# A fused attention and two feed-forward networks: sixteen weight loads issued ahead of the second block's q and k, with weight conversion and attention of block 0 placed anew

## The chip, the core and the metric

The kernel runs on one core of a Trainium2 chip. A core has five engines that run their own instruction streams and wait for each other through semaphores: TensorE (PE in the rows, its weight loads PEld), VectorE (DVE), ScalarE (ACT), GpSimd (POOL) and SyncE (SP), which here issues every DMA. The metric is the device time of one execution in microseconds (us), less is better.

## The reference

Attention over chunks of 64 tokens, a gated network and a second network:

```python
scores = scale * np.matmul(q_c, k_c.transpose(0, 1, 2, 4, 3))      # per chunk of 64, 8 heads
attn = np.exp(scores - np.max(scores, axis=-1, keepdims=True))
attn = attn / (np.sum(attn, axis=-1, keepdims=True) + 1e-09)
x = np.matmul(attn, v_c)                          # reordered to (4608 tokens, 512)
xn = x / np.sqrt(np.mean(x * x, axis=-1, keepdims=True) + 1e-06) * rms_g
g = xn @ w_gate                                   # 512 -> 1536
y = (g / (1.0 + np.exp(-g)) * (xn @ w_val)) @ w_out
h = y @ w_in                                      # 512 -> 2048
out = (h * np.clip(h + 3.0, 0.0, 6.0) / 6.0) @ w_out2
```

## The kernel before

**Blocks and steps.** The 4608 tokens are worked in nine blocks of 512. All nine go through the first network, then all nine through the second. In the first network a block has twelve steps f (0 to 11), one for each 128 columns of the hidden layer, and a step has three thirds, counted by hk from 0 to 35: the gate product (twelve matmuls of 128x512 into bank GB), the val product (twelve, into bank VB), and the down product of the step before (twelve, into four banks). Gate and val each hold one bank, so the gate product of a step can only start when VectorE has read the one before (L689), and a val product when VectorE has read the val before (L694). L580 on ScalarE and L581 on GpSimd split the product of the two into a high and a low part, which the down product of the next step reads.

**Weights.** The weights arrive as 64-bit floats. The matmuls run on a rounded 32-bit format (fp32r), three of them for one exact product: high weight by high input, low weight by high input, high weight by low input. So each weight is first made a 32-bit float by operations on its two words and then split into a high and a low part. The weights of the first network come in 36 pieces of 512 KB, in the order gate 0, val 0, out 0, gate 1 and so on: piece i belongs to step i // 3. A piece passes through five stages: a DMA into a raw tile (L131), `mag` on ScalarE (L138, the magnitude of the high word), `bits` on VectorE (L145, L147, L149, L153, the 32-bit float), `hi` on ScalarE (L160, the high part) and `lo` on GpSimd (L168, the rest). `Prep.step(2)` advances four pairs of pieces by one stage each; `Prep.fill` loads more pieces while the pool `wp` of 36 slots has room. Raw tiles, finished weights and the attention tiles of block 0 share that pool, so a load can wait for an earlier user of its slot.

**Start.** Attention of block 0 (four `Att` objects) and the first fourteen pieces are written out by hand in `START`; sixteen pieces are loaded there. After that, attention for block b + 1 is done inside block b of the first network by two `Pair` objects of 256 tokens each. Pair 2 and Pair 3 belong to block 1, Pair 4 is the first of block 2. `att_hook(b, hk)` places the steps of a pair: `turn` (two transposes of q and k on VectorE, L405 and L406; right after it the q and k of the next pair are loaded with 32 or 64 small DMAs, L391), `scores` (L418), `top`, `less` and `expo`, `total` and `share`, `trans_p` and `out_p`, `values` (L478) and `squares` (L501), then the load of the next v (L401). After two pairs `rms(b + 1)` normalizes the block's input: a matmul, a square root on ScalarE (L517), a reciprocal (L518) and four products (L521) on VectorE. `x_split` then splits the input into XH (L531, ScalarE) and XL (L533, VectorE and GpSimd), which the first gate product of the next block reads.

**What sets the order.** `manual_schedule` keeps the order in which the code is written: each engine takes its instructions in that order, and one that waits holds up all that stand behind it on its engine. SP's DMAs stand in one queue in that order too; besides, each of them waits on the semaphore of the eighth DMA before it, which that DMA sets when it has landed. `prep_hook(b, hk)` places the conversion of the remaining pieces: in block 0 the table `HKA` says in which thirds a step is made. The hooks stand behind each third's product: in third hk, first the matmuls and the VectorE product, then `att_hook`, then `prep_hook`.

Of the kernel before, what the change touches and what calls it, by code (L numbers as in the profile page):

```python
# [36 lines left out]
    square3 mean2 spread1 norm1 spread0 root2 squares3 mean3 wl2 inv2 root3 wh3 hi1 spread2 norm0 inv3 wm5  # L37
    norm2 hi2 lo1 spread3 hi0 lo2 norm3 hi3 lo3 wh4 wm6 lo0 wl3 wb5 wb6 wh5 wl4
""".split()
HKA = [2, 0, 0, 0, 2, 2, 0, 2, 0, 0, 2, 0, 2, 0, 2, 0, 0, 2, 2, 2, 0, 0, 2, 2, 2, 2, 2, 2, 0, 0, 2, 0, 0, 2, 0, 2]  # L40
HKB = [2, 2, 2, 2, 2, 2, 0, 2, 0, 2, 2, 0, 2, 0, 2, 0, 0, 2, 2, 2, 0, 2, 0, 2, 0, 0, 2, 2, 0, 2, 2, 2, 0, 0, 0, 0]


# [1 line left out]
def fused_kernel(  # L45
# [466 lines left out]
    def rms(blk):  # L512

        ps = PS[:, ATT, :]
        nc.tensor.matmul(ps, ones, sqs.pop(blk), start=True, stop=True)
        rt = at_p.tile([128, N], F32, tag="kT", name="rt")
        nc.scalar.activation(rt, ps, AF.Sqrt, scale=1.0 / DM, bias=eps)  # L517
        nc.vector.reciprocal(rt, rt)  # L518
        x = xf[blk]
        for c in range(KD):  # L520
            nc.vector.scalar_tensor_tensor(  # L521
                out=x[:, c, :], in0=x[:, c, :], scalar=g_sb[:, c:c + 1], in1=rt, op0=ALU.mult, op1=ALU.mult
            )
# [5 lines left out]
    def x_split(x):  # L529
        for c in range(KD):  # L530
            nc.scalar.copy(XH[:, c, :], x[:, c, :])  # L531
            e = nc.vector if c % 2 == 0 else nc.gpsimd
            e.tensor_tensor(XL[:, c, :], x[:, c, :], XH[:, c, :].bitcast(F32), op=ALU.subtract)  # L533


    def mm_up(bank, w, xs):
        ps = PS[:, bank, :]
        n = 3 * KD
        i = 0
        for wi, xi in ((0, 0), (1, 0), (0, 1)):  # L540
            for c in range(KD):
                nc.tensor.matmul(  # L542
                    ps, w[:, wi, c * 128:(c + 1) * 128], xs[c][xi], start=(i == 0), stop=(i == n - 1)
                )
                i += 1

    def mm_down_a(w, a, first, last):
        for m in range(KD):
            ps = PS[:, YB + m, :]
            wm = [w[:, z, m * 128:(m + 1) * 128] for z in range(2)]  # L550
            nc.tensor.matmul(ps, wm[0], a[0], start=first, stop=False)  # L551
            nc.tensor.matmul(ps, wm[1], a[0], start=False, stop=False)  # L552
        for m in range(KD):
            nc.tensor.matmul(PS[:, YB + m, :], w[:, 0, m * 128:(m + 1) * 128], a[1], start=False, stop=last)  # L554
# [22 lines left out]
    def split_act(t):  # L577
        hi = ah_p.tile([128, N], F32R, tag="ah", name="ah")
        lo = al_p.tile([128, N], F32R, tag="al", name="al")
        nc.scalar.copy(hi, t)  # L580
        nc.gpsimd.tensor_tensor(lo, t, hi.bitcast(F32), op=ALU.subtract)  # L581
        return hi, lo

    def y_store(b):
        for m in range(0, KD, 2):
            t = st_p.tile([128, 2, N], F32, tag="st", name="yst")
            nc.scalar.copy(t[:, 0, :], PS[:, YB + m, :])
            nc.vector.tensor_copy(t[:, 1, :], PS[:, YB + m + 1, :])
            nc.sync.dma_start(out=yd[b][:, m:m + 2, :], in_=t)
# [13 lines left out]
    def load_x2(b):  # L603
        xf[b] = xf_p.tile([128, KD, N], F32, tag="xf", name="xf")
        nc.sync.dma_start(out=xf[b], in_=yd[b])
# [7 lines left out]
    with tc.manual_schedule():  # L613
        a_pieces = [(kd, f) for f in range(FA) for kd in ("gate", "val", "out")]
        b_pieces = [(kd, f) for f in range(FB) for kd in ("in2", "out2")]

        prep_a, prep_b = Prep(a_pieces), Prep(b_pieces)


        first = [Att(i) for i in range(NTL)]  # L620
        for op in LOADS:
            if op[0] == "w":
                prep_a.load()
            elif op[0] == "q":
                first[int(op[1])].load_qk()
            else:
                first[int(op[1])].load_v()
        for op in START:
            if op[0] == "w":
                prep_a.token(op)  # L630
            else:
                first[int(op[-1])].run(op[:-1])
        sqs.pop(0)
        xf.pop(0)

        nxt = Pair(N // TP)
        nxt.load_qk()
        nxt.load_v()
        state = {"att": nxt}

        def att_hook(b, hk):

            if b + 1 >= NB:
                return
            f, o = divmod(hk, 3)
            t, g = divmod(f, 5)
            a = state["att"]
            if t == N // TP:
                if hk == 3 * f + 1 and g == 0:
                    rms(b + 1)  # L650
                return
            if (g, o) == (0, 1):
                a.run("turn")
                if a.i + 1 < NPR:
                    state["nxt"] = Pair(a.i + 1)
                    state["nxt"].load_qk()
            elif (g, o) == (1, 0):
                a.run("scores")
            elif (g, o) == (1, 1):
                a.run("top", "less", "expo")  # L660
            elif (g, o) == (2, 1):
                a.run("total", "share")
            elif (g, o) == (3, 1):
                a.run("trans_p", "out_p")
            elif (g, o) == (4, 1):
                a.run("values", "out_x", "square", "squares")
                if "nxt" in state:
                    state["att"] = state.pop("nxt")
                    state["att"].load_v()

        def prep_hook(b, hk):
            if b == 0 and not prep_a.done() and HKA[hk]:
                prep_a.step(HKA[hk])
                prep_a.fill(36)
            if b == NB - 1:
                if HKB[hk]:
                    prep_b.step(HKB[hk])
                prep_b.fill(hk)

        for b in range(NB):  # L680
            prev = None
            hk = 0
            if b == NB - 1:
                load_x2(0)
            for f in range(FA):
                mm_up(GB, W["gate", f], xs)
                s = sg_p.tile([128, N], F32, tag="sg", name="sg")
                nc.scalar.activation(s, PS[:, GB, :], AF.Sigmoid)  # L688
                nc.vector.tensor_tensor(s, s, PS[:, GB, :], op=ALU.mult)  # L689
                att_hook(b, hk)  # L690
                prep_hook(b, hk)
                hk += 1
                mm_up(VB, W["val", f], xs)
                nc.vector.tensor_tensor(s, s, PS[:, VB, :], op=ALU.mult)  # L694
                a = split_act(s)
                att_hook(b, hk)
                prep_hook(b, hk)
                hk += 1
                if prev is not None:
                    mm_down_a(W["out", f - 1], prev, f == 1, False)  # L700
                att_hook(b, hk)
                prep_hook(b, hk)
                hk += 1
                prev = a
            if b + 1 < NB:
                x_split(xf.pop(b + 1))
            else:
                x_split(xf.pop(0))
            mm_down_a(W["out", FA - 1], prev, False, True)
            y_store(b)  # L710

        for b in range(NB):
            prev = None
            if b + 1 < NB:
                load_x2(b + 1)
            for f in range(FB):
                bank = GB + f % 2
                if b == 0:
                    prep_b.fill(36)
                    prep_b.step(2)  # L720
                mm_up(bank, W["in2", f], xs)
                s = sg_p.tile([128, N], F32, tag="sg", name="sg")
                nc.scalar.activation(s, PS[:, bank, :], AF.Relu, bias=three)  # L723
                nc.vector.scalar_tensor_tensor(  # L724
                    out=s, in0=s, scalar=6.0, in1=PS[:, bank, :], op0=ALU.min, op1=ALU.mult
                )
                a = split_act(s)
                if prev is not None:
                    mm_down_b(W["out2", f - 1], prev, f == 1, False)
                prev = a  # L730
            if b + 1 < NB:
                x_split(xf.pop(b + 1))
            mm_down_b(W["out2", FB - 1], prev, False, True, b == NB - 1)
            o_store(b)
# [29 lines left out]
```

## Time and profile before

| | us |
|---|---|
| median of 3 runs (1868.18 to 1870.50) | 1869.09 |
| the profiled execution | 1870.38 |
| its span in the trace | 1868.6 |
| TensorE busy in the span | 1782.3 (95%) |
| VectorE, ScalarE, GpSimd busy | 727.0, 601.1, 542.4 |

The profiled execution is 1.3 us over the median, and 1.8 us of it lie outside the span of the trace. TensorE is busy nearly throughout; the slices of the page show its busy share under 90% only in the first five of forty (234 us) and in a short place near the middle where the second network's weights are converted. Block 0 of the first network lies in slices 1 to 4.

### The profile page before, as it was taken

What the parts mean: (1) busy time and instruction counts of PE and PEld (TensorE: products, weight loads), DVE (VectorE), ACT (ScalarE), POOL (GpSimd) and SP (SyncE); (2) the same over time, 40 slices, a digit from 0 to 9 for tenths busy, and PEclk for the clock granted to TensorE, in tenths of its full rate; (3) what the DMA queues carried; (4) which work ended last, traced back from release to release, by engine and by line L of the source; (5) the groups of instructions that cost most, each with busy time, mean ns of one, the idle gap of its engine ahead of it and who ended that gap; (6) DMA issues with size and microseconds to landing.
All of it is one profiled execution on the core that took longest, in us unless ns stands there. A gap on an engine that the chain in (4) does not pass through costs nothing.

```text
span 1868.6 us, 24155 instructions
## 1 busy us (share of the span) xinstructions
PE 1782.3 (95%) x9856; PEld 1457.4 (78%) x9856; DVE 727.0 (39%) x930; ACT 601.1 (32%) x899; POOL 542.4 (29%) x395
## 2 busy tenths in 40 slices
PE   5678999999999999999999889999999999999999
PEld 4556788888888888888887678888888888888887
DVE  7787534344353534335359951121212121212121
ACT  5344423233232323233234432222323232322222
POOL 3534322112121212112125652222223232323222
PEclk8789999999999999999999999999999999999999
DMA  9362211212212121212034410110101010101000
GB/s 249 78 170 70 49 31 44 41 28 49 40 40 45 39 44 26 51 36 46 12 102 153 142 55 1 46 36 10 46 0 46 1 46 1 45 1 46 0 23 23
DMA packets 225199, 93.88 MB, mean 50 GB/s; under 512 B 192960, under 2 KB 213440, under 8 KB 223936
## 3 DMA queue, kind: packets, MB, share of 16 engines
q1 hardware_dynamic: 225088, 92.34, 18.8%
q8 instruction: 77, 1.26, 0.3%
q14 instruction: 34, 0.28, 0.1%
HBM read 73.40 MB, written 18.87 MB: 49 GB/s over the span
## 4 chain that ended last, share of the span: by engine, by line
PE 82%; DVE 6%; SPq 3%; issue 3%; POOL 2%; DMA 2%; ACT 1%; DVEq 0%; POOLq 0%; ACTq 0%
PE PS L542 45%; PE PS L563 7%; PE PS L559 7%; PE PS L560 7%; PE PS L551 4%; PE PS L552 4%; PE PS L554 4%; SPq L391 2%; POOL w L168 2%; DVE wtmp L149 1%; DVE wraw L153 1%; PE PS L418 1%; DMA wraw<-in_moe_w_gate_dram 1%; PE PS L478 1%; DVE wtmp L145 1%
## 5 line engine op out<-in xcount | busy, mean ns | idle before, releaser
L542 PE MATMUL PS<-XH,w 128*128 128x512 f32 x2880 | 729.6, 396 | 41.8 <-DVE sg L689 29.4
L581 POOL TENSOR_TENSOR al<-sg,ah 128x512 fp32r<-128x512 f32 x252 | 334.0, 1325 | 1279.9 <-ACT ah L580 1279.9
L542 PEld LDWEIGHTS PS<-XH,w 128*128 128x128 f32 x2880 | 547.5, 191 | 163.9 <-DVE sg L689 33.7
L542 PE MATMUL PS<-XL,w 128*128 128x512 f32 x1440 | 389.0, 392 | 0.0
L724 DVE SCALAR_TENSOR_TENSOR sg<-sg,PS 128x512 f32<-128x512 f32 x144 | 99.2, 689 | 623.5 <-ACT sg L723 623.5
L542 PEld LDWEIGHTS PS<-XL,w 128*128 128x128 f32 x1440 | 273.8, 190 | 57.7
L580 ACT CAST ah<-sg 128x512 fp32r<-128x512 f32 x252 | 156.3, 620 | 429.6 <-DVE sg L694 313.9
L723 ACT ACTIVATE sg<-PS,three 128x512 f32<-128x512 f32 x144 | 99.1, 688 | 445.8 <-PE PS L542 431.5
L559 PE MATMUL PS<-w,ah 128*128 128x512 f32 x576 | 224.5, 390 | 2.8 <-ACT ah L580 2.8
L560 PE MATMUL PS<-w,ah 128*128 128x512 f32 x576 | 224.1, 389 | 0.0
L689 DVE TENSOR_TENSOR sg<-sg,PS 128x512 f32<-128x512 f32 x108 | 74.0, 685 | 274.7 <-ACT sg L688 274.6
L551 PE MATMUL PS<-ah,w 128*128 128x512 f32 x432 | 175.8, 407 | 0.2 <-ACT ah L580 0.2
L552 PE MATMUL PS<-ah,w 128*128 128x512 f32 x432 | 168.5, 390 | 0.0
L563 PE MATMUL PS<-w,al 128*128 128x512 f32 x576 | 154.9, 390 | 2.1 <-POOL al L581 2.1
L688 ACT ACTIVATE sg<-PS 128x512 f32<-128x512 f32 x108 | 64.4, 596 | 246.1 <-PE PS L542 229.5
L559 PEld LDWEIGHTS PS<-w,ah 128*128 128x128 f32 x576 | 108.1, 188 | 26.4 <-ACT ah L580 4.0
L563 PEld LDWEIGHTS PS<-w,al 128*128 128x128 f32 x576 | 108.2, 188 | 25.2 <-POOL al L581 2.9
L560 PEld LDWEIGHTS PS<-w,ah 128*128 128x128 f32 x576 | 108.2, 188 | 22.4
L694 DVE TENSOR_TENSOR sg<-sg,PS 128x512 f32<-128x512 f32 x108 | 74.2, 687 | 120.5 <-PE PS L542 117.1
L554 PE MATMUL PS<-al,w 128*128 128x512 f32 x432 | 115.8, 390 | 0.1
L168 POOL TENSOR_TENSOR w<-wraw,w 128x512 fp32r<-128x512 f32 x68 | 102.0, 1525 | 17.9 <-ACT w L160 17.9
L551 PEld LDWEIGHTS PS<-ah,w 128*128 128x128 f32 x432 | 81.1, 188 | 21.4 <-ACT ah L580 2.8
(85 smaller groups left out, 1229.0 us busy)
## 6 DMA issues: line engine op xcount, KB each, us to landing
wraw<-in_moe_w_out_dram SPq DMA_DIRECT2D x28, 512.0 KB, 5.2
yd<-yst SPq DMA_DIRECT2D x18, 512.0 KB, 3.4
xf<-yd SPq DMA_DIRECT2D x9, 1024.0 KB, 6.5
wraw<-in_moe_w_in_dram SPq DMA_DIRECT2D x16, 512.0 KB, 3.9
out_dram<-ost SPq DMA_DIRECT2D x16, 512.0 KB, 3.2
wraw<-in_moe_w_gate_dram SPq DMA_DIRECT2D x12, 512.0 KB, 6.5
wraw<-in_moe_w_val_dram SPq DMA_DIRECT2D x12, 512.0 KB, 7.4
v<-in_v_dram SPq DMA_DIRECT2D x96, 64.0 KB, 2.6
```

The lines of the kernel that those rows point to most:

```text
L168: nc.gpsimd.tensor_tensor(w[:, 1, :], self.raw.pop(i)[:, :, 0].bitcast(F32), w[:, 0, :].bitcast(F32), op=ALU.subtract)
L542: nc.tensor.matmul(ps, w[:, wi, c * 128:(c + 1) * 128], xs[c][xi], start=(i == 0), stop=(i == n - 1))
L551: nc.tensor.matmul(ps, wm[0], a[0], start=first, stop=False)
L552: nc.tensor.matmul(ps, wm[1], a[0], start=False, stop=False)
L554: nc.tensor.matmul(PS[:, YB + m, :], w[:, 0, m * 128:(m + 1) * 128], a[1], start=False, stop=last)
L559: nc.tensor.matmul(PS[:, YB + m, :], am, w[:, 0, :], start=first, stop=False)
L560: nc.tensor.matmul(PS[:, YB + m, :], am, w[:, 1, :], start=False, stop=False)
L563: nc.tensor.matmul(PS[:, YB + m, :], a[1][:, m * 128:(m + 1) * 128], w[:, 0, :], start=False, stop=last)
L580: nc.scalar.copy(hi, t)
L581: nc.gpsimd.tensor_tensor(lo, t, hi.bitcast(F32), op=ALU.subtract)
L723: nc.scalar.activation(s, PS[:, bank, :], AF.Relu, bias=three)
L724: nc.vector.scalar_tensor_tensor(out=s, in0=s, scalar=6.0, in1=PS[:, bank, :], op0=ALU.min, op1=ALU.mult)
```

## The change

Three edits, all in block 0 of the first network:

- All weight pieces that fit are loaded at once behind `START` (`fill(36, 36)`), before the q and k of Pair 2; the v of Pair 2 is loaded in third 0.
- `HKA` makes a conversion step in every second third (hk 0, 2, 4, ...), and `fill` is tried in every third.
- Attention of block 0 stands one step (three thirds) later: the first `turn` in third 4 and no longer in third 1, `rms` in third 34 and no longer in 31. The other blocks keep their places.

```diff
-HKA = [2, 0, 0, 0, 2, 2, 0, 2, 0, 0, 2, 0, 2, 0, 2, 0, 0, 2, 2, 2, 0, 0, 2, 2, 2, 2, 2, 2, 0, 0, 2, 0, 0, 2, 0, 2]
+HKA = [0 if hk % 2 else 2 for hk in range(36)]
...
+        prep_a.fill(36, 36)
         nxt = Pair(N // TP)
         nxt.load_qk()
-        nxt.load_v()
         state = {"att": nxt}
...
             f, o = divmod(hk, 3)
+            a = state["att"]
+            if b == 0:
+                if hk == 0:
+                    a.load_v()
+                    return
+                f -= 1
             t, g = divmod(f, 5)
-            a = state["att"]
+            if t < 0:
+                return
             if t == N // TP:
-                if hk == 3 * f + 1 and g == 0:
+                if o == 1 and g == 0:
                     rms(b + 1)
                 return
...
-            if b == 0 and not prep_a.done() and HKA[hk]:
-                prep_a.step(HKA[hk])
+            if b == 0 and not prep_a.done():
+                if HKA[hk]:
+                    prep_a.step(HKA[hk])
                 prep_a.fill(36)
```

Line numbers in the changed code from `att_hook` on are 8 higher (L689 becomes L697, L694 becomes L702).

SP's queue behind the last load of `START`, one piece of the difference (- before, + after); `wraw` are weight pieces, q, k and v those of the pairs:

```order
-L391 DMA q<-in_q_dram 32x2x32 x16
-L391 DMA q<-in_q_dram 32x6x32 x16
-L391 DMA k<-in_k_dram 32x2x32 x16
-L391 DMA k<-in_k_dram 32x6x32 x16
-L401 DMA v<-in_v_dram 64x64 x8
-L401 DMA v<-in_v_dram 64x3x64 x8
 L131 DMA wraw<-in_moe_w_val_dram 128x4x256
```

```order
+L131 DMA wraw<-in_moe_w_out_dram 128x1024
+L131 DMA wraw<-in_moe_w_gate_dram 128x4x256
+L131 DMA wraw<-in_moe_w_val_dram 128x4x256
+L391 DMA q<-in_q_dram 32x2x32 x16
+L391 DMA q<-in_q_dram 32x6x32 x16
+L391 DMA k<-in_k_dram 32x2x32 x16
+L391 DMA k<-in_k_dram 32x6x32 x16
```

The 64 DMAs for q and k of Pair 2 stood in front of the next weight piece; now sixteen pieces stand in front of them (the last three are shown).

VectorE in the first two steps of block 0, before:

```order
L689 TENSOR_TENSOR sg<-sg,PS 128x512
L694 TENSOR_TENSOR sg<-sg,PS 128x512
L405 STREAM_TRANSPOSE qT<-q 128x1024
L406 STREAM_TRANSPOSE kT<-k 128x1024
L689 TENSOR_TENSOR sg<-sg,PS 128x512
L694 TENSOR_TENSOR sg<-sg,PS 128x512
```

and after, the same place:

```order
L697 TENSOR_TENSOR sg<-sg,PS 128x512
L702 TENSOR_TENSOR sg<-sg,PS 128x512
L145 TENSOR_SCALAR wtmp<-wtmp 128x512 x2
L147 TENSOR_SCALAR wtmp<-wtmp 128x512 x2
L149 SCALAR_TENSOR_TENSOR wtmp<-wraw,wtmp 128x512 x2
L153 SCALAR_TENSOR_TENSOR wraw<-wraw,wtmp 128x512 x2
L697 TENSOR_TENSOR sg<-sg,PS 128x512
L702 TENSOR_TENSOR sg<-sg,PS 128x512
L405 STREAM_TRANSPOSE qT<-q 128x1024
L406 STREAM_TRANSPOSE kT<-k 128x1024
```

The transposes moved behind the products of step 1, and a pair of pieces is converted in front of them. From these transposes to those of Pair 3 VectorE has the same ten products L689 and L694 before and after, and six conversions of a pair before, eight after.

## Rows read from the trace of the kernel before

**Rows 1.** Busy time by stretch: stretch, length, busy us of each engine (instructions), PEclk, DMA, GB/s.
```profile
60.00:212.00 152.00, 117.50 (x694) 91.85 (x693) 113.29 (x149) 62.48 (x93) 64.05 (x44) 0.90 0.37 98
212.00:318.40 106.40, 106.06 (x707) 86.80 (x706) 44.84 (x52) 33.71 (x46) 22.62 (x17) 1.00 0.20 40
```
**Rows 2.** Waits in 60 to 212 us: who waited for whom, us in total, times, longest.
```profile
PE PS L542 <- DVE sg L689: 27.2, 7, 6.7
```
**Rows 3.** SP in order of time: start us, us until the last issue, issues.
```profile
40.55 19.58 SPq L391 DMA_DIRECT2D q<-in_q_dram  x32
60.17 15.50 SPq L391 DMA_DIRECT2D k<-in_k_dram  x32
...
141.96 16.28 SPq L391 DMA_DIRECT2D q<-in_q_dram  x32
158.34 15.08 SPq L391 DMA_DIRECT2D k<-in_k_dram  x32
173.60 0.35 SPq L131 DMA_DIRECT2D wraw<-in_moe_w_out_dram  x1
```
**Rows 4.** Chain of work that ended last, in order of time: start us, us, what.
```profile
40.14 7.13 DMA wraw<-in_moe_w_gate_dram
...
75.23 1.94 DMA k<-in_k_dram
77.19 1.26 DVE kT L406
78.49 1.99 PE PS L418 x64
...
117.46 10.15 DMA wraw<-in_moe_w_gate_dram
...
212.35 2.72 PE PS L542 x12
```
**Rows 5.** GpSimd in order of time, end of the start stretch: start us, us, what.
```profile
57.41 6.33 POOL L168 TENSOR_TENSOR w<-wraw,w 128x512 fp32r<-128x512 f32 x4
```
**Rows 6.** VectorE in order of time, block 0: start us, us, what [idle before <- releaser].
```profile
85.00 0.69 DVE L694 TENSOR_TENSOR sg<-sg,PS 128x512 f32<-128x512 f32 x1 [5.99 <-PE PS L542]
...
88.06 2.66 DVE L145 TENSOR_SCALAR wtmp<-wtmp 128x512 f32<-128x512 f32 x2
...
95.96 0.75 DVE L145 TENSOR_SCALAR wtmp<-wtmp 128x512 f32<-128x512 f32 x2
...
99.82 0.69 DVE L689 TENSOR_TENSOR sg<-sg,PS 128x512 f32<-128x512 f32 x1
...
115.30 0.69 DVE L689 TENSOR_TENSOR sg<-sg,PS 128x512 f32<-128x512 f32 x1 [3.62 <-ACT sg L688]
...
140.69 1.24 DVE L405 STREAM_TRANSPOSE qT<-q 128x1024 f32<-128x1024 f32 x1
...
189.40 0.67 DVE L689 TENSOR_TENSOR sg<-sg,PS 128x512 f32<-128x512 f32 x1
...
201.10 3.35 DVE L518 RECIPROCAL rt<-rt 128x512 f32<-128x512 f32 x1 [2.69 <-ACT rt L517]
204.49 2.74 DVE L521 SCALAR_TENSOR_TENSOR xf<-xf,g_sb,rt 128x512 f32<-128x512 f32 x4
...
209.83 3.14 DVE L533 TENSOR_TENSOR XL<-xf,XH 128x512 fp32r<-128x512 f32 x2 [1.21 <-ACT XH L531]
```
**Rows 7.** ScalarE in order of time, block 0: start us, us, what [idle before <- releaser].
```profile
112.64 0.66 ACT L138 ACTIVATE wtmp<-wraw 128x512 f32<-128x512 f32 x1 [9.55 <-DMA wraw<-in_moe_w_out_dram]
...
178.94 0.67 ACT L138 ACTIVATE wtmp<-wraw 128x512 f32<-128x512 f32 x1 [8.83 <-DMA wraw<-in_moe_w_out_dram]
...
181.01 0.60 ACT L580 CAST ah<-sg 128x512 fp32r<-128x512 f32 x1
```
**Rows 8.** TensorE in order of time, block 0: start us, us, what [idle before <- releaser].
```profile
80.41 3.63 PE L542 MATMUL PS<-XH,w 128*128 128x512 f32 x8
...
190.13 3.41 PE L542 MATMUL PS<-XH,w 128*128 128x512 f32 x8 [3.43 <-DVE sg L689]
```

## The prediction

> **What bounds the kernel now.** I read the stretches first. After block 0 the first network is TensorE at full clock: 106.06 us busy in 106.40, granted clock 1.00 [rows 1]; no edit touches those blocks. Block 0 has 117.50 us of TensorE work in 152, at 0.90, and VectorE is busy for 113.29 of it. So the change can only act there, and the reader is to see that VectorE, not TensorE, sets the pace: the table of waits has 27.2 us in seven waits of TensorE for L689 [rows 2], which stands on VectorE behind the conversions. Next the chain of waits shows what VectorE and ScalarE wait for in turn: SP's issue of small DMAs. The k of Pair 2 lands at 75.23 + 1.94 = 77.17 and its transpose starts at 77.19 [rows 4], though 64 DMAs for q and k were begun at 40.55 [rows 3]. ScalarE waits 9.55 and 8.83 us for weight pieces [rows 7] that stand in SP's queue behind the q and k of Pairs 3 and 4. The change moves exactly this queue, so I follow one path through block 0 with four markers: K, the k of Pair 2 transposed (77.19 + 1.26 = 78.45 before); X, the transposes of Pair 3 begin (140.69, [rows 6]); Y, piece 32 has landed and ScalarE takes it up (178.94, [rows 7]); E, block 1's first gate product begins (212.35, [rows 4]).
>
> **Term 1, to K: 16 pieces in front of q and k.** SP now issues sixteen pieces before the first q. Two things can hold them: their slots, and the DMA engines. Slots first: the last two wait for the first two of the four subtractions that start at 57.41 and take 6.33 [rows 5], so until about 60.6. The DMA engines hold longer: the last piece of the start lands at 40.14 + 7.13 = 47.27 [rows 4]. For the rate I take the twelve pieces that are now loaded together: ScalarE gets the first of them at 112.64 [rows 7], and the eleventh lands at 117.46 + 10.15 = 127.61 [rows 4]; 14.97 us for ten pieces, 1.50 each. The sixteenth then lands at 47.27 + 24.0 = 71.3. The eighth q waits on that piece's semaphore by the order, so the small DMAs can't overtake in effect: after it 56 of 64 are still to be issued. Before, the same queue took from 47.27 to 77.19 for the same work, and I shift that by 24.0: the transpose of k starts at 101.2 and K is 102.4. VectorE is there by then: with nothing but two products and one conversion behind 70 it arrives some 20 us early, and TensorE, whose scores stand behind the gate product of step 2, idles about as long. Term 1: +24.0. Bounds: the slots alone give 60.6 + 64 issues of 15.50/32 = 0.48 + 1.9 to land = 93.5, +16.3 (no wait for data at all); the sixteen pieces of the start, with every q, k and v between them, took 47.27, so +47. The twelve loads are the nearer row, since nothing stands between them either.
>
> [...]
>
> **Term 2, K to X: VectorE's list.** Before, this took 140.69 - 78.45 = 62.2 us, of which VectorE idled 5.99 for the cold val product and 3.62 for the late ScalarE [rows 6]. After, the order has the same ten products and attention steps between the two pairs' transposes, but eight conversions of a pair and not six; the first idle time goes, since two conversions stand in front of val's product, the second too, since pieces 16 to 31 have landed. A conversion that runs alone takes 99.82 - 95.96 = 3.86 us; one beside GpSimd's subtractions 95.96 - 88.06 = 7.90 [rows 6]. GpSimd has the same twelve `lo` and the same splits in this stretch as before, so I charge the two extra conversions at 3.86: +7.7 - 9.6 = -1.9, X at K + 60.3. Bounds: both slow, +6.2; if all eight ran alone, the list would also lose the excess of three slow ones of before, 3 x 4.0, so -14.
>
> **Term 3, X to Y: unchanged, and now it bites.** The q and k of Pair 4 go out when Pair 3's are transposed: 64 issues from 141.96 to 173.42, then pieces 32 to 35 from 173.60 [rows 3], landed for ScalarE at 178.94. That is 38.25 after X, and the order has the same queue there afterwards. But the transposes now stand in third 19 and no longer in 16, while ScalarE asks for piece 32 in third 24 either way, in front of the split of step 8. Before it had 29.4 us of other work and waited 8.83. After it has five thirds, about 13 us with the scores, and waits some 25; TensorE runs on through val 8, down 7, gate 9 and val 9 and then idles about 17 us for the split, L580 (181.01 before, [rows 7]). Term 3: 0.0 on this path, since it was on SP all along; the new waits are the price of arriving early.
>
> **Term 4, Y to E: a gain and a loss that cancel.** Before, two conversions stand in front of step 9's product L689 at 189.40, which opens gate 10 at 190.13 [rows 6, 8]; after only one does, -3.8, and gate 10 starts some 7.4 after Y. Behind it come three losses. The clock: after a long idle a product's first eight matmuls take 3.63 and not the 1.8 that full speed gives (two thirds of 2.72) [rows 4, 8]; most of this falls on down 8, which has slack, +0.4. The `values` of Pair 3 now stand behind gate 10; 64 such matmuls took 1.99 cold [rows 4], so +1.1 warm. And `rms` moves from third 31 to 34, so nothing is left to hide it: from the end of val 11 run product 0.7, then 2.69 until the reciprocal, 3.35, 2.74 for the four products, 3.14 for XL, and two last matmuls 0.5 [rows 6], together 13.1 until the first gate product of block 1 can end; TensorE alone would need three products of 2.72 and a half us for rms, 8.7. A stall of 4.4. Less 2.3 for stalls and slow matmuls of gate 10 to down 11 that were there before (212.35 - 190.13 = 22.2, against seven products of 2.72 and some 0.9 for rms). Term 4: -3.8 + 0.4 + 1.1 + 4.4 - 2.3 = -0.2. Bounds: -4.6 if the stall of `rms` is hidden, +3 if the clock stays low for longer.
>
> **The sum.** 24.0 - 1.9 + 0.0 - 0.2 = +21.9 us on E. From E on all blocks are equal in both orders. The profiled execution, 1870.4, becomes 1892.3; the median, 1.3 below it, 1891.0. About 0.2% (3.7 us) is what a measurement of this kernel can tell from no change.
>
> **Rivals.** *VectorE's conversions run alone.* If the even spacing puts them beside GpSimd's idle time, X comes up to 12 us earlier: 1879. For it: VectorE converts the first pairs while GpSimd has nothing. Against: each step puts four `lo` or splits beside two conversions. 0.13. *q and k come at the slots' time*, not behind 24 us of data: -7.7, 1883. Against it is the semaphore of the eighth DMA. 0.05. *The loads run slower beside the start's traffic*, +7 and more: 1898 to 1902. 0.10. *Not slower: TensorE and not VectorE becomes the bound from K to X.* The place is the list of term 2. TensorE has there scores and thirteen products of 2.72, with attention and cold clock about 42 us, so the price is 18.3, 1872.7, within 0.2%. It decides from the point where VectorE's list is under 42, which needs eight conversions at under 2 us, half of what one alone takes [rows 6]; 0.04, of which 0.01 falls under 1865. *The change doesn't do what it says*: were pieces 16 to 31 held by slots far past 60.6, q and k would come later still; the gains of term 2 don't depend on it, and its time lies with the slower loads.
>
> **How the numbers follow.** Forecast 0.68, which spans 1885 to 1897 by terms 2 and 4. With 0.13 at 1879 and above, 0.05 at 1883, 0.10 up to 1902 and 0.04 at 1873 the range 1878 to 1901 leaves out under 0.2: the tails of the forecast, a part of the slow loads, and the last rival. Slower by over 0.2%: 0.94; the same: 0.05; faster: 0.01.
>
> **What would show it.** Right: the transpose of Pair 2's k starts near 101, with VectorE idle some 20 us for a DMA of k, and TensorE idle as long before the scores; about 60 us to Pair 3's transposes; ScalarE waits about 25 us for piece 32; block 1 begins near 234, its first gate product waiting for XH and XL; from there blocks of 106.4. Wrong: k lands before 95, or the wait for piece 32 is under 10 us, or blocks after block 0 differ in length.

## The result and the profile after

The changed kernel took 1890.63 us (1889.93 to 1892.97) where the kernel before took 1868.63 (1867.31 to 1870.5) on the same chip: a ratio of 1.0119 with an interval of 1.0102 to 1.0137, 22.0 us slower. The profiled execution shown here took 1889.93 us with a span of 1888.1; the one of before 1870.38 with 1868.6. The two spans differ by 19.5, the medians by 22.0; the sums below go by the spans and by times within them.

Two stretches of the changed kernel, block 0 and the first block after it (columns as in [rows 1]: stretch, length, busy us of each engine with its instructions, granted clock, DMA share, GB/s):

```profile
60.00:235.00 175.00, 123.49 (x712) 98.11 (x711) 113.00 (x152) 63.34 (x95) 67.88 (x46) 0.82 0.25 59
235.00:341.40 106.40, 106.06 (x707) 86.77 (x706) 44.92 (x51) 33.70 (x45) 22.70 (x16) 1.00 0.18 35
```

From block 1 on nothing changed: TensorE is busy for 106.06 us in 106.40 at a granted clock of 1.00, the same as in [rows 1]. VectorE's work in block 0 is also what it was, 113.00 us against 113.29. What grew is the idle time around it, and TensorE's mean granted clock over block 0 fell from 0.90 to 0.82; it was busy 123.49 us in place of 117.50 for nearly the same instructions.

The waits of block 0 (54 to 236 us; who waited for whom, us in total, times, longest) name the new idle time:

```profile
PE PS L460 <- POOL p L454: 19.1, 1, 19.1
PE PS L418 <- DVE kT L406: 17.1, 2, 15.0
...
DVE kT L406 <- DMA k<-in_k_dram: 13.9, 1, 13.9
PE PS L542 <- DVE sg L697: 12.9, 3, 7.1
```

TensorE's waits for the gate step L697 (L689 before) fell from 27.2 us in seven [rows 2] to 12.9 in three. The even conversions go with that: in the runs below this wait totals 16.3 us where they stand with the early pieces (`no_shift`) and 21.9 where they stand alone (`even_only`), but 27.0 and 30.8 with the old conversions and one of the other edits (`fill_only`, `att_only`). But two single waits, 19.1 and 15.0 us, came in their place: the first ends when GpSimd has made the shares of Pair 3, the second when k of Pair 2 is transposed.

### The profile page after: what moved, and what is told of

Read it like the earlier page. It is cut to its first block, busy times and chain, and to the rows that moved or that the text cites. A ratio compares the mean times of both kernels' runs of the same rounds, so it can differ in the third digit from the quotient of the medians.

```text
span 1888.1 us, 24147 instructions
## 1 busy us (share of the span) xinstructions
PE 1784.1 (94%) x9856; PEld 1459.9 (77%) x9856; DVE 726.4 (38%) x930; ACT 601.5 (32%) x899; POOL 541.1 (29%) x395
## 4 chain that ended last, share of the span: by engine, by line
PE 82%; DVE 6%; SPq 4%; issue 3%; POOL 2%; DMA 2%; ACT 1%; DVEq 0%; POOLq 0%; ACTq 0%
PE PS L542 45%; PE PS L563 7%; PE PS L560 7%; PE PS L559 7%; PE PS L551 5%; PE PS L552 4%; PE PS L554 4%; SPq L391 3%; DVE wtmp L149 2%; DVE wraw L153 1%; POOL w L168 1%; POOL al L581 1%; PE PS L478 1%; PE PS L418 1%; PE PS L460 1%
## 5 line engine op out<-in xcount | busy, mean ns | idle before, releaser
L580 ACT CAST ah<-sg 128x512 fp32r<-128x512 f32 x252 | 156.4, 621 | 427.8 <-DVE sg L702 312.8
L697 DVE TENSOR_TENSOR sg<-sg,PS 128x512 f32<-128x512 f32 x108 | 74.1, 686 | 278.5 <-ACT sg L696 278.5
L702 DVE TENSOR_TENSOR sg<-sg,PS 128x512 f32<-128x512 f32 x108 | 74.2, 687 | 119.7 <-PE PS L542 116.5
L551 PEld LDWEIGHTS PS<-ah,w 128*128 128x128 f32 x432 | 81.7, 189 | 21.1 <-ACT ah L580 2.2
```

## The path through block 0, before and after

The prediction's markers are K (k of Pair 2 transposed), X (Pair 3's transposes begin) and Y (ScalarE takes up piece 32). For the end I use V, the start of block 1's first `val` product, because in the changed kernel the gate product in front of it is stretched by a stall. The prediction named the start of that gate product, E (212.35 before [rows 4], 228.94 after), but its sum counts the stall that lies within the product, and so reaches to V. TensorE at V in the kernel before:

```profile
214.91 1.98 PE L542 MATMUL PS<-XH,w 128*128 128x512 f32 x8
```

SP in the changed kernel, in order of time (start us, us until the last issue, issues):

```profile
45.24 0.37 SPq L131 DMA_DIRECT2D wraw<-in_moe_w_gate_dram  x1
45.72 1.28 SPq L131 DMA_DIRECT2D wraw<-in_moe_w_val_dram  x1
47.10 2.10 SPq L131 DMA_DIRECT2D wraw<-in_moe_w_out_dram  x1
...
60.54 0.37 SPq L131 DMA_DIRECT2D wraw<-in_moe_w_gate_dram  x1
61.99 0.37 SPq L131 DMA_DIRECT2D wraw<-in_moe_w_val_dram  x1
...
157.70 16.35 SPq L391 DMA_DIRECT2D q<-in_q_dram  x32
174.15 15.97 SPq L391 DMA_DIRECT2D k<-in_k_dram  x32
190.22 0.36 SPq L131 DMA_DIRECT2D wraw<-in_moe_w_out_dram  x1
```

The chain of waits at the start of block 0 (start us, us, what):

```profile
59.07 2.91 POOL w L168 x2
61.99 6.99 DMA wraw<-in_moe_w_val_dram
...
95.61 1.72 DMA k<-in_k_dram
97.35 1.25 DVE kT L406
```

The last two of the sixteen pieces were issued late because of their slots: SP issues them at 60.54 and 61.99, the second of them right when GpSimd's two subtractions end. The chain goes back through that issue, but the slots did not set the landing: the DMA engines were busy for 0.99 of the time from 47 to 69 us, with the pieces in front. The last piece lands at 61.99 + 6.99 = 68.98, the rest of the issues of q and k follows, and K is 97.35 + 1.25 = 98.60, 20.1 us after the 78.45 of before [rows 4].

VectorE, ScalarE, GpSimd and TensorE at the decisive places of the changed kernel, each in order of time (start us, us, what, idle before it and what ended that):

```profile
97.35 1.25 DVE L406 STREAM_TRANSPOSE kT<-k 128x1024 f32<-128x1024 f32 x1 [13.94 <-DMA k<-in_k_dram]
...
156.44 1.23 DVE L405 STREAM_TRANSPOSE qT<-q 128x1024 f32<-128x1024 f32 x1
...
202.26 0.68 DVE L697 TENSOR_TENSOR sg<-sg,PS 128x512 f32<-128x512 f32 x1
```
```profile
193.86 0.66 ACT L138 ACTIVATE wtmp<-wraw 128x512 f32<-128x512 f32 x1 [21.83 <-DMA wraw<-in_moe_w_out_dram]
...
195.93 0.60 ACT L580 CAST ah<-sg 128x512 fp32r<-128x512 f32 x1
```
```profile
196.67 1.27 POOL L581 TENSOR_TENSOR al<-sg,ah 128x512 fp32r<-128x512 f32 x1 [26.79 <-ACT ah L580]
197.91 2.08 POOL L454 TENSOR_TENSOR p<-p,rs 128x1024 f32<-128x1024 f32 x1
```
```profile
200.04 1.97 PE L460 MATMUL PS<-ident,p 128*128 128x128 f32 x8 [19.10 <-POOL p L454]
...
205.59 1.98 PE L542 MATMUL PS<-XH,w 128*128 128x512 f32 x8
...
228.94 0.49 PE L542 MATMUL PS<-XH,w 128*128 128x512 f32 x1 [1.95 <-ACT XH L531]
...
234.66 2.05 PE L542 MATMUL PS<-XH,w 128*128 128x512 f32 x8
```

Read as a relay, the four fences tell one story. ScalarE stands for 21.83 us in front of piece 32, where it stood for 8.83 before [rows 7], because SP issues it at 190.22, behind 64 small DMAs for a pair that nobody needs before block 1. The split of step 8 stands behind that on ScalarE; `al` of step 8 behind the split on GpSimd; the shares of Pair 3 behind `al` on the same engine; and TensorE's transposes of the shares, which stand ahead of `down` 8, behind those. So TensorE idles for 19.10 us. At the end of block 0 the first gate product of block 1 waits 1.95 us for the normalised columns, and then goes on matmul by matmul as they come.

| | before | after | step | forecast of the step | measured |
|---|---|---|---|---|---|
| K | 78.45 | 98.60 | to K | +24.0 | +20.15 |
| X | 140.69 | 156.44 | K to X | -1.9 | -4.40 |
| Y | 178.94 | 193.86 | X to Y | 0.0 | -0.83 |
| V | 214.91 | 234.66 | Y to V | -0.2 | +4.83 |
| sum | | | | +21.9 | +19.75 |

V explains the whole time, within some 2 us. Over the thirteen different kernels of this study (before, after and eleven of the twelve runs below; the twelfth repeats a kernel) the span less V lies between 1651.8 and 1654.1 us, while V itself runs from 194.15 to 238.84.

## The experiments

Each run is given as its median, with the ratio to the kernel before measured beside it. Three groups of runs were made. The first undoes parts of the change or moves its transfers; the second takes the edits one at a time; the third settles what was left.

### Late q and k of Pair 4, and early q and k of Pair 2

My account says that both new waits are q and k standing in a queue on the wrong side of weight pieces. Two moves test that. `late_qk4` lets Pair 4's q and k out only in third 22, behind pieces 32 to 35:

```diff
                     state["nxt"] = Pair(a.i + 1)
-                    state["nxt"].load_qk()
+                    if b > 0 or a.i == N // TP:
+                        state["nxt"].load_qk()
...
                 prep_a.fill(36)
+            if b == 0 and hk == 22:
+                state["nxt"].load_qk()
```

> The changed kernel, with the 64 small DMAs for Pair 4's q and k issued in third 22, behind pieces 32 to 35, and not in third 19 in front of them. Theory (ScalarE's wait for piece 32 behind these DMAs is the second loss): ScalarE's wait of 21.8 us falls under 4, TensorE's idle time of 19.1 us in front of trans_p goes, block 1 begins some 17 us earlier: 1873 (1870 to 1877). Rival (TensorE's 19.1 us come from share and the split on GpSimd, or the time is spent on the conversions anyway): over 1885.

Measured: 1869.58 us, ratio 0.9999 (0.9989 to 1.0008). This one move gives back the whole loss, 21 us where I had expected 17, just under the range that I had given. SP and TensorE of this run (columns as above):

```profile
159.60 0.36 SPq L131 DMA_DIRECT2D wraw<-in_moe_w_out_dram  x1
```
```profile
207.57 4.49 PE L542 MATMUL PS<-XH,w 128*128 128x512 f32 x8 [1.95 <-ACT XH L531]
```

Piece 32's slot is free at 159.60; in the changed kernel it left at 190.22, 30.6 us later, for no other reason than the 64 issues in front of it. With the piece there in time K and X stand as in the changed kernel (k transposed at 97.15, X 156.23), but from X to V it takes 57.33 us and not 78.22, and V is 213.56, 21.1 us earlier. The stall for the normalised columns stays.

`qk_first` puts the q and k of Pair 2 ahead of the twelve pieces:

```diff
-        prep_a.fill(36, 36)
         nxt = Pair(N // TP)
         nxt.load_qk()
+        prep_a.fill(36, 36)
```

> The changed kernel, with the q and k of Pair 2 issued in front of the sixteen pieces and not behind them. Theory (the 24 us of weight data in front of q and k are the first loss): the transpose of k no longer waits some 14 us for its DMA; instead ScalarE waits some 6 us for piece 16 in third 2, since the pieces now start at about 76. K (k of Pair 2 transposed) near 87 and no longer 98.6, and everything behind it moves along: 1879 (1876 to 1883). Rival (the loss comes from the even conversions on VectorE and the attention one step later, the late k being covered by work): within 3 us of the changed kernel, 1888 to 1893.

Measured: 1881.08 us, ratio 1.0059 (1.0044 to 1.0074): about half of the loss. Pair 2 is now transposed at 83.21 and 84.37 and X is 147.13, but ScalarE pays for it, since pieces 16 and 17 are the late ones now; and the second wait is still there in full (ScalarE and TensorE):

```profile
79.34 0.66 ACT L138 ACTIVATE wtmp<-wraw 128x512 f32<-128x512 f32 x1 [8.22 <-DMA wraw<-in_moe_w_val_dram]
```
```profile
191.41 1.97 PE L460 MATMUL PS<-ident,p 128*128 128x128 f32 x8 [18.91 <-POOL p L454]
```

`both` makes the two moves together (the two diffs above).

> Both moves of the two kernels before at once. Theory: the two losses lie one after the other on one path, so the gains add: about 11 + 17 us off the changed kernel, 1862 (1858 to 1867), under the kernel before. Rival (one loss hides the other): no better than the better of the two alone.

Measured: 1858.91 us, ratio 0.9937 (0.992 to 0.9954), 11 us faster than the kernel before. The moves add: 9.6 and 21.1 us under the changed kernel's median by themselves, 31.7 together. So the two waits cost more than the change loses, and with both moves it is worth some 11 us. Some 4 of these the move of Pair 4's q and k gives on the kernel before as well (`late_only` below).

### The attention step of the second half, and two pieces

`both_rms31` is `both` with Pair 3's attention back in the thirds of before, which puts the norm (`rms`) back into third 31, where step 11 still hides it:

```diff
-                f -= 1
+                if hk == 16:
+                    a.run("values", "out_x", "square", "squares")
+                    state["att"] = a = state.pop("nxt")
+                    a.load_v()
+                elif hk < 16:
+                    f -= 1
```

> Both moves, and Pair 3's attention back in the thirds of the kernel before (turn in third 16, rms in third 31), while Pair 2's stays one step later. Theory: the stall at block 1's first product, where rms stands in the last step and nothing hides it (predicted 4.4 us), goes: 4 to 5 us under the kernel with both moves, 1857 (1853 to 1862). Rival (that stall was covered, or comes back on VectorE as attention meets the conversions): the same as both moves, within 1.5 us, or slower.

Measured: 1853.38 us, ratio 0.9911 (0.9896 to 0.9926). Gate 10 begins at 172.90 here and at 173.00 in `both`, but V is 197.07 against 201.62: 4.55 us, which is the size of the stall. The wait for the normalised columns is gone and TensorE's last small wait in block 0 is another (TensorE of `both_rms31`):

```profile
191.50 0.50 PE L551 MATMUL PS<-ah,w 128*128 128x512 f32 x1 [1.24 <-ACT ah L580]
```

The same kernel was run again beside the next one:

> The fastest kernel so far once more, beside the one with two pieces ahead of q and k on the same chip: 1853.4 (1852 to 1855.5).

Measured: 1853.64 us, ratio 0.9908 (0.9892 to 0.9925).

In `both_rms31` ScalarE still waits 4.73 us for piece 16 and 0.63 for piece 17. `two_first` puts just pieces 16 and 17 back in front of Pair 2's q and k:

```diff
+        prep_a.fill(36, 2)
         nxt = Pair(N // TP)
         nxt.load_qk()
         prep_a.fill(36, 36)
```

> The fastest kernel so far (q and k of Pair 2 ahead of the twelve pieces, those of Pair 4 behind pieces 32 to 35, Pair 3's later steps and the norm in the thirds of before) with pieces 16 and 17 ahead of Pair 2's q and k. Theory: ScalarE's waits of 4.7 and 0.6 us for those two go, while k lands about 3 us later: 1851 (1848 to 1855). Rival (k is the bound there, not ScalarE): 1853 to 1857.

Measured: 1849.36 us (1848.26 to 1850.23), ratio 0.9882 (0.9868 to 0.9897), the fastest kernel of the study: 22.6 us under the kernel before, measured beside it. Its q and k cost VectorE nothing any more (VectorE, and TensorE at V):

```profile
79.66 1.25 DVE L406 STREAM_TRANSPOSE kT<-k 128x1024 f32<-128x1024 f32 x1 [0.24 <-issue]
...
131.69 1.24 DVE L405 STREAM_TRANSPOSE qT<-q 128x1024 f32<-128x1024 f32 x1
```
```profile
194.15 1.98 PE L542 MATMUL PS<-XH,w 128*128 128x512 f32 x8
```

k is transposed about when VectorE comes to it, X is 9 us earlier than before, and nothing waits for piece 32; ScalarE's wait is down to 2.01 us, for piece 18. The rival, k as the bound, is out: the time lies under its range and under every run of `best_again` beside it (1851.77 to 1855.21), and k's transpose came 3.45 us earlier than in `both_rms31` (83.11), where ScalarE's late piece had held up the gate step in front of it. Of these, 1.7 us are the start of block 0, which stood at 54.10 here and at 55.82 there.

### One edit at a time

Each of these is the kernel before with one of the change's three edits (the diffs are cut at `...`).

```diff
+        prep_a.fill(36, 36)
         nxt = Pair(N // TP)
```

> The kernel before with one of the three edits alone: the first network's pieces 12 to 17 are issued ahead of the second block's q, k and v; conversions and attention stand as before. Theory (64 small transfers in SP's order are the price): k lands some 20 us later, as in the kernel after, and everything up to Pair 3's transposes goes with it; ScalarE's two waits of about 9 us for pieces go where the pieces are early, but piece 32, which now comes behind Pair 4's q and k, is asked for by ScalarE some 8 us too soon. Time 1886 (1881 to 1890). Rival (early weights are a gain in themselves, since ScalarE no longer waits): under 1866.

The pieces that this moves ahead are 16 to 31, not 12 to 17. Measured: 1889.34 us, ratio 1.0098 (1.0083 to 1.0113), as the theory had it. VectorE and ScalarE:

```profile
98.40 1.25 DVE L406 STREAM_TRANSPOSE kT<-k 128x1024 f32<-128x1024 f32 x1 [13.69 <-DMA k<-in_k_dram]
...
157.58 1.24 DVE L405 STREAM_TRANSPOSE qT<-q 128x1024 f32<-128x1024 f32 x1
```
```profile
194.46 0.66 ACT L138 ACTIVATE wtmp<-wraw 128x512 f32<-128x512 f32 x1 [7.44 <-DMA wraw<-in_moe_w_out_dram]
```

K, X and Y are those of the changed kernel to within 1.2 us. The early pieces alone carry the late path; ScalarE waits only 7.44 us for piece 32, since it comes to it later than in the changed kernel, but the piece is as late.

```diff
-HKA = [2, 0, 0, 0, 2, 2, 0, 2, 0, 0, 2, 0, 2, 0, 2, 0, 0, 2, 2, 2, 0, 0, 2, 2, 2, 2, 2, 2, 0, 0, 2, 0, 0, 2, 0, 2]
+HKA = [0 if hk % 2 else 2 for hk in range(36)]
...
-            if b == 0 and not prep_a.done() and HKA[hk]:
-                prep_a.step(HKA[hk])
+            if b == 0 and not prep_a.done():
+                if HKA[hk]:
+                    prep_a.step(HKA[hk])
                 prep_a.fill(36)
```

> The kernel before with the conversions alone moved to every second third of a step; issue order and attention as before. Theory: ScalarE asks for piece 16 in third 2, at about 74 us, while it lands behind the second pair's q, k and v at about 90, and for piece 20 in third 6 while it lands at about 112: two waits in front of everything that ScalarE does for the gates, together 10 us or less at the end. Time 1876 (1871 to 1882). Rival (even spacing costs nothing and takes TensorE's waits for converted weights away): within 3 us of the kernel before.

Measured: 1877.51 us, ratio 1.0036 (1.0023 to 1.0049), as the theory had it. ScalarE asks for piece 16 long before it lands, and waits another 6.83 us for piece 20:

```profile
89.64 0.66 ACT L138 ACTIVATE wtmp<-wraw 128x512 f32<-128x512 f32 x1 [15.76 <-DMA wraw<-in_moe_w_val_dram]
```

The third edit, attention one step later:

```diff
-        nxt.load_v()
...
+            if b == 0:
+                if hk == 0:
+                    a.load_v()
+                    return
+                f -= 1
             t, g = divmod(f, 5)
...
+            if t < 0:
+                return
             if t == N // TP:
-                if hk == 3 * f + 1 and g == 0:
+                if o == 1 and g == 0:
```

> The kernel before with attention alone one step later in block 0; issue order and conversions as before. Theory: k of the second pair lands as before, Pair 3's transposes begin a step later, piece 32 behind Pair 4's q and k some 37 to 38 us after that, and the stop at block 1's first gate for the normalised columns is added. Time 1883 (1877 to 1888). Rival (attention has slack in block 0): within 3 us of the kernel before.

Measured: 1893.83 us, ratio 1.0124 (1.0109 to 1.0139), 11 us above my forecast and above its range. VectorE and TensorE:

```profile
156.04 1.23 DVE L405 STREAM_TRANSPOSE qT<-q 128x1024 f32<-128x1024 f32 x1
```
```profile
199.53 1.97 PE L460 MATMUL PS<-ident,p 128*128 128x128 f32 x8 [20.52 <-POOL p L454]
```

Here X is 15.35 us later than before, because one more step, three thirds, stands in front of Pair 3's transposes; Y is 193.35, and from Y to V it takes 45.49 us, 9.5 more than before. 15.35 - 0.94 + 9.5 = 23.9. I had the delay of X too small, and I had not counted that, with the conversions of before, two of them still stand in front of step 9's product.

The three edits alone cost 19.3, 7.5 and 23.8 us, 50.6 together; the change costs 22.0. They don't add because two of them arrive at the same place: X is 157.58 with the early pieces alone, 156.04 with the late attention alone, 156.44 with everything. Whichever of the two is there, Pair 3's transposes begin some 16 us late, and the q and k of Pair 4 leave then. The even conversions cost their 7.5 while pieces 16 and up are late; with the early pieces they gain some 4 us, as `no_shift` below shows against `fill_only`: the times are 1885.25 and 1889.34, with ratios whose intervals overlap, but V is 228.97 against 233.98 in the traces.

### What the attention step costs within the change, and what TensorE waits for

`no_shift` is the changed kernel with attention in the thirds of before (and `load_v` beside `load_qk` again):

```diff
+        nxt.load_v()
...
-            a = state["att"]
-            if b == 0:
-                if hk == 0:
-                    a.load_v()
-                    return
-                f -= 1
...
-            if t < 0:
-                return
+            a = state["att"]
             if t == N // TP:
-                if o == 1 and g == 0:
+                if hk == 3 * f + 1 and g == 0:
```

> The kernel after with attention in block 0 back in the thirds of before; early pieces and even conversions stay. Theory: k lands as late as in the kernel after, Pair 3's transposes begin at about 157 us and piece 32 some 37 us behind them, all as there; but share and transposes of the shares now stand ahead of ScalarE's wait for piece 32, and the reciprocal of the norm has cover again, so only the 5 us of those two come back: 1884.5 (1881 to 1888). Rival (the attention step carries a part of the price by itself, as it does alone on the kernel before): 1870 to 1877.

Measured: 1885.25 us, ratio 1.0076 (1.0061 to 1.0091), as the theory had it. ScalarE at Y and TensorE at V:

```profile
193.47 0.66 ACT L138 ACTIVATE wtmp<-wraw 128x512 f32<-128x512 f32 x1 [11.07 <-DMA wraw<-in_moe_w_out_dram]
```
```profile
228.97 1.98 PE L542 MATMUL PS<-XH,w 128*128 128x512 f32 x8
```

X is 155.95 and Y 193.47, as in the changed kernel; V is 228.97. From Y to V it takes 35.50 us, where the changed kernel takes 40.80 and the kernel before 35.97. So beside the early pieces the later attention step costs 5.3 us behind Y and 0.4 ahead of it, and not the 23.8 that it costs alone.

`ask25` moves only ScalarE's question for piece 32 in the changed kernel, from third 24 to third 25:

```diff
-HKA = [0 if hk % 2 else 2 for hk in range(36)]
+HKA = [2 if hk == 25 or hk % 2 == 0 and hk != 24 else 0 for hk in range(36)]
```

> The kernel after with the two conversions of step 8's last pieces (piece 32 the first of them) asked for one third of a step later (third 25 in place of 24). Theory: TensorE's 19 us of idle time in front of Pair 3's transposes of the shares end with GpSimd's share, which stands behind the split of step 8 and so behind ScalarE's wait for piece 32. With the wait one third later, share, transposes and the down products of step 8 run while the piece is under way, and TensorE waits at step 9's split or gate instead: about 3 us less, 1887.4 (1885 to 1889.5). Rival (only the landing of the piece counts, whatever stands in front of it): 1890.6, within 1.5 us of the kernel after.

Measured: 1887.37 us, ratio 1.009 (1.0073 to 1.0107), 3.3 us under the changed kernel's median, though the two ratios' intervals overlap. The trace decides more clearly than the time. GpSimd, ScalarE and TensorE:

```profile
178.32 1.91 POOL L454 TENSOR_TENSOR p<-p,rs 128x1024 f32<-128x1024 f32 x1 [0.40 <-DVE rs L449]
```
```profile
195.17 0.66 ACT L138 ACTIVATE wtmp<-wraw 128x512 f32<-128x512 f32 x1 [18.68 <-DMA wraw<-in_moe_w_out_dram]
```
```profile
183.07 1.03 PE L460 MATMUL PS<-ident,p 128*128 128x128 f32 x8
...
201.52 3.78 PE L542 MATMUL PS<-XH,w 128*128 128x512 f32 x8 [14.68 <-DVE sg L697]
```

The shares are made at 178.32 and not at 197.91, the transposes and `down` 8 run while the piece is still under way, and TensorE's one long wait ends with step 9's L697. Gate 10 begins 6.35 us after Y and not 11.73. Part of that is paid back by its slow first matmuls (3.78 us for eight, 1.98 in the changed kernel, where other matmuls had run first); from Y to V it is 37.78, 3.0 less.

### The late transfer without the rest of the change

`late_only` is the kernel before with the move of `late_qk4`, one third later, since pieces 32 to 35 are issued there:

```diff
-                    state["nxt"].load_qk()
+                    if b > 0 or a.i == N // TP:
+                        state["nxt"].load_qk()
...
+            if b == 0 and hk == 23:
+                state["nxt"].load_qk()
```

> The kernel before with one thing changed: q and k of Pair 4 are issued behind pieces 32 to 35 and not ahead of them. Theory: ScalarE's wait of 8.83 us for piece 32 goes, and block 1 begins some 7 us earlier: 1862.5 (1859 to 1867). Rival (VectorE's list or another wait takes its place): within 3 us of the kernel before.

Measured: 1867.36 us, ratio 0.998 (0.9971 to 0.9989): about 4 us under the kernel before, where I had expected 7 and more; that is over my range, and past the 3 us of the rival. GpSimd, SP and ScalarE of this run:

```profile
169.68 5.11 POOL L168 TENSOR_TENSOR w<-wraw,w 128x512 fp32r<-128x512 f32 x4
```
```profile
171.02 0.35 SPq L131 DMA_DIRECT2D wraw<-in_moe_w_out_dram  x1
```
```profile
174.72 0.66 ACT L138 ACTIVATE wtmp<-wraw 128x512 f32<-128x512 f32 x1 [4.75 <-DMA wraw<-in_moe_w_out_dram]
```

GpSimd in the kernel before:

```profile
169.83 5.10 POOL L168 TENSOR_TENSOR w<-wraw,w 128x512 fp32r<-128x512 f32 x4
```

Piece 32's slot comes free only at 171.0 here, during GpSimd's four subtractions, and these stand at the same place in the kernel before; there q and k of Pair 4 held the piece until 173.60 [rows 3], 2.6 us longer. So of the wait of 8.83 us of before [rows 7] some 4 went with the queue, and 4.75 stay without it: the slot, and the 3.7 us from issue to landing. Only in the changed kernel, where the slot is free at about 159.6 (`late_qk4`), is the wait nearly all queue. The early pieces and even conversions do bring something, then: room that the order of transfers had hidden. `two_first` uses it.

## Why the prediction was right, and where its steps were not

The forecast of 1891.0 was met within half a microsecond, and that closeness is luck. The steps up to Y came 7.2 us shorter than forecast and the last one 5.0 us longer; what is left, 19.75 in the two profiled executions against 21.9, is made up by the difference between executions, since the medians differ by 22.0. The direction and the mechanism, q and k behind weight pieces and then a weight piece behind q and k, are shown: `late_qk4` and `both` remove the loss by moving only those transfers, and `fill_only` makes most of it. Of the signs that the prediction named, k's transpose came at 97.35 (101 forecast), K to X took 57.84 us (60), ScalarE waited 21.83 us (25), block 1's first gate product waited for the normalised columns and began at 228.94 (near 234 forecast, which is V, 234.66), and the blocks behind it are unchanged.

**Term 1, +24.0 forecast, +20.15 measured.** The path was the forecast one, pieces, small issues, k, and as I had written it is the DMA engines and not the slots that hold the pieces. The sixteen land one behind the other, from 46.2 (the last piece of the start, issued at 39.04) to 69.0, 1.43 us apart, also where the last two were issued late. `ask25` has the same program up to third 24; there these two were issued 2.0 us earlier, at 58.58 and 59.99, and the last landed at 69.9, 0.9 us later. What was off is the size, by 3.9 us: 1.1 since the last piece of the start landed that much earlier than before (47.27), 1.2 since a piece took 1.43 and not 1.50, and 1.6 between the last landing and k's transpose, 28.4 us, for which I had shifted the 29.9 of before. VectorE waited 13.94 us for k, behind 2.0 for q, and TensorE 14.96, in place of the 20 forecast. Neither rival on this term came, q and k at the slots' time or slower loads.

**Term 2, -1.9 forecast, -4.40 measured.** Within the bounds; the list of VectorE ran 2.5 us shorter. The eight conversions took 40.2 us where six had taken 36.1, so the two extra ones cost 4.2 and not 7.7: three were long in either kernel (5.67, 9.84 and 5.98 now, 7.89, 7.62 and 9.31 before), and the others took 3.75 each. Against that the waits fell by 7.8 and not 9.6, since one of 1.81 for ScalarE remained; the other 0.8 lie in the instructions between. The rival that needed all conversions to run alone, 12 us earlier, came in this small part only, and that TensorE becomes the bound from K to X didn't come.

**Term 3, 0.0 forecast, -0.83 measured.** Right. SP's 64 issues and the piece behind them take what they took; X to Y was 36.9 to 37.7 us in `fill_only`, `att_only`, `no_shift` and `ask25` too. Its new wait on ScalarE was forecast at 25 and was 21.83.

**Term 4, -0.2 forecast, +4.83 measured.** This step failed, in its first half. I let gate 10 begin 7.4 us after Y, because only one conversion stands in front of step 9's product. L697 was indeed done by 202.94, 9.1 after Y, but TensorE was not there: gate 10 began at 205.59, 11.7 after Y (before: 190.13, 11.2 after Y). I had written that TensorE idles for the split, L580. It idles for GpSimd's shares, which stand two instructions behind that split on another engine, and then it still has the transposes and `down` 8 to do. So the gain of 3.8 us that I booked was a loss of 0.5. `ask25` shows it by letting the shares run ahead of the wait. The second half, from gate 10 to V, was forecast at +3.6 (0.4 + 1.1 + 4.4 - 2.3) and was +4.3 (29.07 against 24.78); `no_shift` shows that the later attention step accounts for the whole excess behind Y, and `both` against `both_rms31` gives 4.55 us for the stall of the norm with Pair 3's steps, where the forecast had 4.4.

**The price of the second wait.** The prediction called the new wait for piece 32 the price of arriving early. That was too mild: it is a price of its own, and the larger one. Term 3 came out as 0.0 because the same 64 issues stood in front of that piece before too, where without them it would have waited for its slot until 171.0 (`late_only`). With the slot free at about 159.6 the change could have had a gain there of some 17 us (X to V 57.33 in `late_qk4`, 74.22 before) and left it in SP's queue. The sum hid that the change gives and takes: some 32 us lost in two waits, and 11 gained once both are gone.

Not settled: what part of the loss is the clock. It was not separated from the idle time that goes with it; the mean granted clock of block 0 is 0.82 in the changed kernel, 0.91 in `two_first` (60 to 200 us).

## What to carry to other kernels

A queue that issues in order is a resource like an engine: 64 small transfers cost SP some 32 us in this kernel, and whoever stands behind them waits that long, though the DMA engines were busy for only 0.21 of that time (158 to 190 us). Before loading something earlier or issuing it sooner, list what now stands behind it in that queue and when each of those is asked for; order by the time of need, not by the time at which a slot is free. And when a wait moves, follow it through every engine's own order to the instruction with which the bound engine really restarts: here that was two engines further than the one that waited for the transfer.

## What the runs showed of the hardware that I had not expected

Issuing is not equally cheap. One weight piece of 512 KB took SP 0.36 us to issue at 190.22, behind no other piece; in the row of pieces at 45 to 49 us the same kind of instruction took 0.37, 1.28 and 2.10, and the three took 4.05 us until the next began. A queue that is still busy with earlier pieces may hold the issuing engine; that was not tried. The landings of these pieces stand 1.43 us apart on average, so here the uneven issues did not set the pace.

The start differs from one execution to the next before the change can act: block 0's first gate product begins at 54.33 in the profile of before and at 56.41 in that of `even_only`, at 55.97 in that of the changed kernel and at 53.95 in that of `ask25`, and the programs of each two are the same up to there. Some 2 us in a difference of two spans can be this alone, which is why the steps behind K are taken between markers of one execution; K itself, and every marker that is compared by its time from the span's start, can hold such a difference.
